# Staging the last weight matrix of a fused attention and gated-MLP kernel in three buffers instead of one

## The chip, the cores and the metric

The kernel runs on one core of one Trainium2 chip. The metric is the device time in microseconds (us) of that core. TensorE is called PE in the profile, VectorE DVE, ScalarE ACT, GpSimd POOL and SyncE SP; PEld is TensorE's weight load.

## The reference

Causal attention over 8 batches and 8 heads (576 positions, head size 64), with a bias from the running sum of `max(s, 0)`, and behind it a gated MLP. With `x` the attention's output, 512 wide:

```python
h = np.maximum(x @ w_in, 0.0)              # 512 -> 1024
u, v = h[..., :512], h[..., 512:]
v_n = (v - mean(v)) / sqrt(var(v) + 1e-6)  # over the last axis
v_s = einsum('ts,bsd->btd', w_spatial, v_n) + b_spatial[None, :, None]
return (u * v_s) @ w_out                   # 512 -> 512
```

The weights `w_in` and `w_out` arrive as 64-bit floats. This document is about how `w_out` (512 x 512) gets into the form in which the last product reads it.

## The kernel before, in words

**The precision scheme.** A matrix product is made of three float16 products: each operand is held as a high part and a low part (the rest that the high part leaves, also float16), and high x high, high x low and low x high are summed in one PSUM bank. So `w_out` is held as `wo1` (high) and `wo2` (low), each four pieces of 128 rows.

**How a piece of w_out is made** (`load_wout`, lines 496 to 498). `fetch_w64` brings 128 x 512 64-bit numbers (512 KB) by a DMA that is issued from GpSimd's queue. `split_w64` (lines 469 to 478) then works on the two 32-bit halves: three integer operations on VectorE build a 32-bit float in a scratch tile `t`; ScalarE squares the upper word in place, so that a fourth VectorE operation can zero tiny numbers; `split_w` (lines 458 to 464) makes the high part on ScalarE. For the low part `split_w` has two ways, chosen by its last argument: with True, one VectorE operation multiplies and subtracts; with False, ScalarE scales the scratch in place and GpSimd subtracts. `load_wout` passes False.

**The tiles.** The 64-bit words of all four pieces are staged in the one tile `WST`, which before that serves a piece of `w_in` and, in `load_wtail`, a small bias row. The scratch `t` comes from `OB`, a ring of two tiles that is handed out in program order: the four pieces of `w_spatial` (`load_wsp`) use it just before the pieces of `w_out`, the output tiles of the MLP after them. `PH` is a ring of two tiles that hold softmax weights of the pairs of heads from number 8 on (in the profile they are called `pb`); before that nothing uses them here.

**What orders the work.** There is no loop order in the program: every operation is recorded with a priority, and a planner in the kernel file (`Recorder.forward`, line 199) plays the whole program through with estimated durations, on each engine always taking the ready operation with the lowest priority number. The result is a fixed order for each engine's queue, and on the chip each engine goes through its queue in that order and waits where something is not there yet. An operation that has nothing to wait for can be placed long before its number suggests, as soon as its engine has nothing lower to do. [...] The numbers: the attention scores of pair p (two heads) start at 2p - 1, its weighted sum at 2p + 2.7; the MLP of batch b is 29 units between 8b + 10.3 and 8b + 18.3; evacuations of the MLP come 3 earlier than their unit. `w_in` has 0.1 to 7.5, `w_spatial` 8.3 to 9.7, and the four pieces of `w_out` 10.6, 11.7, 12.8 and 13.9.

**The last product of a batch** (lines 863 to 883) has 8 units of 12 matmuls, for 128 output rows and half of the positions each. A unit takes the next of three PSUM banks `psM` in turn and is cut into two halves of 6 matmuls: the first half needs the pieces 0 and 1 of `w_out`, the second half the pieces 2 and 3. The same three banks, in the same turn, serve the other three products of the MLP, the transposes of softmax weights (`ident,p` in the profile) and the division by the softmax sums (`over`, `smx` and `rb` in the profile, pairs 0 to 7), without which the MLP of the next batch has no input.

Of the kernel before, what the change touches and what calls it, by code (L numbers as in the profile page):

```python
# [10 lines left out]
U32 = mybir.dt.uint32  # L11
# [288 lines left out]
def attn_gated_mlp(ctx, tc, qkT, v, s, w_in, w_spT, b_sp, w_out, outT):  # L300
    nc = tc.nc
    P = 128
# [7 lines left out]
    w_out = w_out.bitcast(U32)  # L310
    NF = FF // 2
# [18 lines left out]
    def tiles(n, shape, dt, name):  # L330
        return [cp.tile(shape, dt, name=f"{name}{i}") for i in range(n)]
# [19 lines left out]
    WST = tiles(1, [P, 2 * NF], U32, "wst")[0]  # L351
# [3 lines left out]
    PH = Ring(tiles(2, [P, 2 * 1280], F16, "pb"))  # L355
# [11 lines left out]
    wo1, wo2 = (cp.tile([P, FC, DM], F16, name=n) for n in ("wo1", "wo2"))  # L367
# [90 lines left out]
    def split_w(dst1, dst2, raw, sc, dve):  # L458
        A.activation(dst1, raw, AF.Copy, bias=0.0, scale=sc)
        if dve:  # L460
            V.scalar_tensor_tensor(out=dst2, in0=raw, scalar=sc, in1=dst1, op0=ALU.mult, op1=ALU.subtract)
            return
        A.activation(raw, raw, AF.Copy, bias=0.0, scale=sc)
        G.tensor_tensor(out=dst2, in0=raw, in1=dst1, op=ALU.subtract)

    def fetch_w64(src, st):
        G.dma_start(out=st, in_=src)

    def split_w64(dst1, dst2, st, t, dve):
        st = st.rearrange("p (f two) -> p f two", two=2)  # L470
        lo, hi = st[:, :, 0], st[:, :, 1]
        V.tensor_scalar(t, hi, 0x07FFFFFF, 3, op0=ALU.bitwise_and, op1=ALU.logical_shift_left)
        V.scalar_tensor_tensor(out=t, in0=hi, scalar=0xC0000000, in1=t, op0=ALU.bitwise_and, op1=ALU.bitwise_or)
        V.scalar_tensor_tensor(out=t, in0=lo, scalar=29, in1=t, op0=ALU.logical_shift_right, op1=ALU.bitwise_or)
        sq, tf = hi.bitcast(F32), t.bitcast(F32)
        A.activation(sq, sq, AF.Square, bias=0.0, scale=1.0)
        V.scalar_tensor_tensor(out=tf, in0=sq, scalar=2.0 ** -30, in1=tf, op0=ALU.is_ge, op1=ALU.mult)
        split_w(dst1, dst2, tf, SW, dve)
# [9 lines left out]
    def wt():  # L488
        return OB.next()[:, 0:NF].bitcast(U32)

    def load_win(hf, c):
        t = HV.next().bitcast(U32) if hf else wt()
        split_w64(win1[:, c, hf * NF:(hf + 1) * NF], win2[:, c, hf * NF:(hf + 1) * NF], STG[hf, c], t,
                  c < (2 if hf else 1))

    def load_wout(c):
        fetch_w64(w_out[c * P:c * P + P], WST)
        split_w64(wo1[:, c], wo2[:, c], WST, wt(), False)

    def load_wsp(c):  # L500
        st = OB.next()
# [388 lines left out]
    def at(pos, d, fn, *args):  # L890
        plan.append((pos, len(plan), d, fn, args))
# [42 lines left out]
    for c in range(KC):  # L934
        at(0.1 + 0.5 * c if c < 2 else 1.5 + 0.1 * c, 0, fetch_win, 1, c)
        at(2.1 + 0.5 * c if c < 3 else 4.05, 0, fetch_win, 0, c)
        at(2 + 1.0 * c, 0, load_win, 1, c)
        at(6 + 0.5 * c, 0, load_win, 0, c)
        at(8.5 + 0.4 * c, 0, load_wsp, c)
        at(10.6 + 1.1 * c, 0, load_wout, c)  # L940
    at(8.3, 0, load_wtail)
    for p in range(NP):
        units([2 * p + k / 3 for k in range(6)], ATT, s_pass, p)
# [46 lines left out]
```

## Time and profile before

| | |
|---|---|
| median of 3 runs | 661.55 us (661.17 to 663.3) |
| profiled execution | 661.49 us |
| its span in the trace | 659.8 us |
| PE busy | 620.2 us, 94% |
| DVE busy | 527.2 us, 80% |
| ACT busy | 505.9 us, 77% |
| POOL busy | 214.3 us, 32% |
| DMA, mean rate | 161 GB/s |

The profiled execution spends 1.69 us outside its span. The profile cuts the span into 40 slices of 16.5 us and gives the busy tenths of each engine and the clock that TensorE was granted. The kernel records all its operations through one helper, so nearly every row carries the line number 279: rows are told apart by the names of their tiles (`psM<-g,wo` is a matmul of the last product; `wst`, `ob`, `wo` belong to the making of `w_out`). An entry such as [1.68 <-ACT q] behind a row is the time that the engine sat idle before it, and what released it.

### The profile page before, as it was taken

To read this page: it belongs to the slowest core of one execution; us is meant where nothing else is said; L and a number is where in the kernel's file an instruction comes from. 1 tells how busy PE (TensorE), PEld (TensorE's weight loads), DVE (VectorE), ACT (ScalarE), POOL (GpSimd) and SP (SyncE) were. 2 spreads that over 40 slices of the span, in tenths; PEclk is the share of its full clock that TensorE was granted. 3 is DMA by queue.
4 is the path that set the end of the run, shared out by engine and by line. 5 is a ranking of instruction groups with operands and counts; after the bars stand their busy time and mean duration, and the time that the engine had idled before them with its cause. 6 is when DMAs were issued, how large, how long until landed. Compare 5 with 4: busy or idle time off the path is not lost.

```text
span 659.8 us, 15930 instructions
## 1 busy us (share of the span) xinstructions
PE 620.2 (94%) x5785; PEld 426.7 (65%) x5785; DVE 527.2 (80%) x1527; ACT 505.9 (77%) x1336; POOL 214.3 (32%) x326
## 2 busy tenths in 40 slices
PE   6983779999689999999999999999999999999997
PEld 3542455777456776677757775677667775777675
DVE  8788787868867898999889988999899988880440
ACT  3895987988866889798879888788889897862422
POOL 9746545542332413432243323323243112000200
PEclk9995999999799999999999999999999999999999
DMA  8854355342992899898998999998999895762001
GB/s 222 266 180 125 111 144 151 104 122 87 197 240 57 198 193 243 176 176 183 241 208 180 197 210 206 180 197 186 238 174 204 160 209 92 107 116 74 12 2 72
DMA packets 185574, 106.20 MB, mean 161 GB/s; under 512 B 162025, under 2 KB 165271, under 8 KB 185497
## 3 DMA queue, kind: packets, MB, share of 16 engines
q1 hardware_dynamic: 176201, 70.14, 53.4%
q0 software_dynamic: 9296, 35.07, 18.4%
q8 instruction: 45, 0.74, 0.5%
q14 instruction: 32, 0.26, 0.1%
HBM read 37.48 MB, written 9.66 MB: 71 GB/s over the span
## 4 chain that ended last, share of the span: by engine, by line
PE 82%; ACT 7%; DVE 5%; DMA 2%; issue 2%; POOL 2%; SPq 0%; ACTq 0%; DVEq 0%; POOLq 0%
PE psM L279 60%; PE psS L279 12%; PE psV L279 8%; ACT p L279 2%; PE psT L279 2%; DVE psS L279 1%; DMA raw<-in_qkT_dram 1%; ACT pT L279 1%; DMA st<-st 1%; POOL QB L279 1%; DVE hv L279 1%; ACT q L279 1%; ACT KA L279 1%; DVE g L279 1%; DVE mx L279 1%
## 5 line engine op out<-in xcount | busy, mean ns | idle before, releaser
L279 DVE CUSTOM_DVE_ANT_0 psS<-psS,mb 128x128 f32<-128x128 f32 (+1 forms) x320 | 155.2, 497 | 29.3 <-PE psS L279 24.7
L279 ACT ACTIVATE p<-psS,mx 128x128 f32<-128x128 f32 (+3 forms) x256 | 134.4, 530 | 42.1 <-DVE mx L279 38.8
L279 POOL TENSOR_TENSOR QB<-raw,KA 128x288 f16<-128x288 f32 x116 | 89.8, 797 | 142.1 <-ACT KA L279 141.4
L279 DVE SCALAR_TENSOR_TENSOR pb<-p,sm,pb 128x384 f16<-128x384 f32 x192 | 103.5, 572 | 6.9 <-ACT pb L279 6.2
L279 PE MATMUL psM<-ws,vn 128*128 128x288 f16 x768 | 106.0, 286 | 0.0
L279 PE MATMUL psM<-g,wo 128*128 128x288 f16 x768 | 103.3, 289 | 0.5 <-POOL wo L279 0.5
L279 PE MATMUL psM<-xt,win 128*128 128x288 f16 x768 | 101.4, 286 | 0.1
L279 PE MATMUL psM<-win,xt 128*128 128x512 f16 (+1 forms) x576 | 100.7, 344 | 0.0
L279 ACT ACTIVATE pb<-p,sm 128x384 f16<-128x384 f32 x192 | 96.2, 560 | 1.0 <-ACT p L279 0.5
L279 PEld LDWEIGHTS <-wo 128*128 128x128 f16 x768 | 74.9, 99 | 26.2 <-issue 2.8
L279 PEld LDWEIGHTS <-win 128*128 128x128 f16 x768 | 73.9, 98 | 23.4 <-issue 2.1
L279 PE MATMUL psS<-KA,QA 128*128 128x128 f16 (+1 forms) x348 | 80.4, 306 | 9.0 <-ACT p L279 5.4
L279 PEld LDWEIGHTS <-vn 128*128 128x128 f16 x768 | 74.0, 98 | 22.7 <-issue 1.6
L279 PE MATMUL psS<-KB,QB 128*128 128x128 f16 (+1 forms) x348 | 87.2, 300 | 0.0
L279 PEld LDWEIGHTS <-xt 128*128 128x128 f16 (+1 forms) x576 | 46.4, 102 | 45.5 <-issue 4.2
L279 PE MATMUL psV<-pT,vv 128*64 128x384 f16 (+5 forms) x880 | 64.5, 298 | 5.6 <-DVE hv L279 5.6
L279 POOL TENSOR_SCALAR rs<-mv 128x1 f32<-128x1 f32 x40 | 12.7, 318 | 146.4 <-DVE mv L279 145.5
L279 PEld LDWEIGHTS <-vv 128*64 128x64 f16 x1440 | 45.5, 111 | 13.8 <-issue 6.1
L279 ACT ACTIVATION_READ_ACCUMULATOR p<-psS,mx 128x1 f32 x256 | 52.3, 204 | 0.0
L279 ACT CAST g<-g 128x288 f16<-128x288 f32 x64 | 27.5, 431 | 27.6 <-DVE g L279 27.4
L279 DVE DVE_READ_ACCUMULATOR2_ANT mx<- 128x1 f32 x320 | 44.8, 140 | 0.0
L279 PEld LDWEIGHTS <-QA 128*128 128x128 f16 x348 | 28.9, 101 | 21.5 <-issue 14.3
(124 smaller groups left out, 951.6 us busy)
## 6 DMA issues: line engine op xcount, KB each, us to landing
raw<-in_qkT_dram POOLq DMA_DIRECT2D x29, 576.0 KB, 5.3
out_dram<-ob SPq DMA_DIRECT2D x32, 288.0 KB
vraw<-in_v_dram POOLq DMA_DIRECT2D x12, 512.0 KB, 5.7
QA<-KA SPq DMA_DIRECT2D x29, 144.0 KB
KB<-KA SPq DMA_DIRECT2D x29, 144.0 KB
KB<-QB SPq DMA_DIRECT2D x29, 144.0 KB
QB<-KA SPq DMA_DIRECT2D x29, 144.0 KB
vv<-in_v_dram POOLq DMA_DIRECT2D x4, 512.0 KB, 7.5
```

The costliest lines, as they stand in the source:

```text
L279: getattr(eng, method)(*args, **kw)
```

## The change

It moves the transfers of `w_out` into a function of their own, gives the four pieces three staging buffers (pieces 0 and 3 the first tile of `PH`, piece 1 the second, piece 2 `WST`), gives the transfers the numbers 10, 10.3, 10.6 and 10.9 and the conversions 10.5, 11.2, 11.9 and 12.6, and makes all four low parts on VectorE.

```diff
+    def stage_out(c):
+        return WST if c == 2 else PH.tiles[c % 3].bitcast(U32)[:, 0:2 * NF]
+
+    def fetch_wout(c):
+        fetch_w64(w_out[c * P:c * P + P], stage_out(c))
+
     def load_wout(c):
-        fetch_w64(w_out[c * P:c * P + P], WST)
-        split_w64(wo1[:, c], wo2[:, c], WST, wt(), False)
+        split_w64(wo1[:, c], wo2[:, c], stage_out(c), wt(), True)
...
-        at(10.6 + 1.1 * c, 0, load_wout, c)
+        at(10 + 0.3 * c, 0, fetch_wout, c)
+        at(10.5 + 0.7 * c, 0, load_wout, c)
```

## The prediction

> **What bounds the kernel now.** I read the page's strip first. Each digit is 16.5 us; the eleventh and twelfth slices (165 to 198 us) are the last with a PE below 9 before the end, and the eleventh has a lowered clock.
>
> ```profile
> PE   6983779999689999999999999999999999999997
> ...
> PEclk9995999999799999999999999999999999999999
> ```
>
> Then the windows: busy us (and instructions) of PE, PEld, DVE, ACT and POOL, the granted clock, the DMA share and GB/s.
>
> ```profile
> 98.00:159.00 61.00, 60.69 (x494) 42.94 (x493) 47.81 (x136) 49.77 (x131) 27.61 (x42) 1.00 0.45 126
> 159.00:186.00 27.00, 20.05 (x158) 12.67 (x155) 22.63 (x69) 23.57 (x60) 10.92 (x14) 0.87 0.78 165
> 186.20:655.70 469.50, 469.39 (x4619) 328.70 (x4618) 376.73 (x1110) 359.30 (x944) 114.61 (x185) 1.00 0.78 162
> ```
>
> PE is full from 98 to 159 and has 0.11 us of idle time in the 469.5 us from 186.2 to the end. So what is saved before 186 moves the end one for one, unless a new idle time opens behind it. Between lie 27 us with 6.95 us idle. The timeline of PE there:
>
> ```profile
> 159.09 2.37 PE L279 MATMUL psM<-g,wo 128*128 128x288 f16 x18
> ...
> 167.30 0.38 PE L279 MATMUL psS<-KA,QA 128*128 128x512 f16 x1 [1.68 <-ACT q L279]
> ...
> 171.23 0.26 PE L279 MATMUL psS<-KA,QA 128*128 128x128 f16 x1 [2.88 <-ACT p L279]
> ...
> 174.80 5.71 PE L279 MATMUL psM<-g,wo 128*128 128x288 f16 x37 [0.51 <-POOL wo L279]
> ...
> 185.64 0.38 PE L279 MATMUL psS<-KA,QA 128*128 128x512 f16 x1 [1.80 <-ACT q L279]
> ...
> 186.16 1.50 PE L279 MATMUL psM<-win,xt 128*64 128x256 f16 x24
> ```
>
> The 18 matmuls at 159.09 are three first halves of units (3 x 6); they leave all three psM banks half summed. The waits that follow name attention (ACT q, ACT p), but that is only what came next in PE's queue. What is missing is the rest of the last product, as the windows of tile psM alone show:
>
> ```profile
> 161.50:172.80 11.30, 0.00 (x0) 0.00 (x0) 0.00 (x0) 0.00 (x0) 0.88 0.62 140
> ```
>
> For 11.3 us no instruction touches those banks. The piece that they wait for is seen on POOL:
>
> ```profile
> 104.32 0.60 POOL L279 DMA_DIRECT2D wst<-in_w_out_dram  x1
> ...
> 127.27 0.61 POOL L279 DMA_DIRECT2D wst<-in_w_out_dram  x1
> ...
> 129.96 1.15 POOL L279 TENSOR_TENSOR wo<-ob,wo 128x512 f16<-128x512 f32 x1 [0.44 <-ACT ob L279]
> ...
> 141.98 0.53 POOL L279 DMA_DIRECT2D wst<-in_w_out_dram  x1 [6.40 <-DVE ob L279]
> ...
> 155.98 0.53 POOL L279 DMA_DIRECT2D wst<-in_w_out_dram  x1 [6.58 <-DVE ob L279]
> 157.54 1.16 POOL L279 TENSOR_TENSOR wo<-ob,wo 128x512 f16<-128x512 f32 x1 [1.04 <-ACT ob L279]
> ...
> 173.11 1.63 POOL L279 TENSOR_TENSOR wo<-ob,wo 128x512 f16<-128x512 f32 x1 [4.28 <-ACT ob L279]
> ```
>
> One staging tile makes a relay: each transfer waits for the conversion before it, and the fourth low part ends at 174.74. The chain of waits runs through it and straight on into PE:
>
> ```profile
> 173.11 1.64 POOL wo L279
> ...
> 174.80 7.62 PE psM L279 x53
> ```
>
> The lowered clock sits behind the same gap:
>
> ```profile
> 168.00:171.00 3.00, 0.35 (x2) 0.16 (x2) 3.00 (x8) 3.00 (x9) 0.57 (x1) 0.84 0.92 160
> 171.00:174.00 3.00, 2.77 (x11) 1.34 (x10) 3.00 (x8) 2.16 (x7) 0.89 (x1) 0.50 0.88 270
> 174.00:177.00 3.00, 2.49 (x12) 1.43 (x11) 2.67 (x11) 2.73 (x9) 2.02 (x3) 0.52 1.16 207
> ```
>
> PE worked 2.77 us at 0.50 and 2.49 us at 0.52; at full clock that is 2.77 x 0.50 + 2.49 x 0.48 = 2.6 us less.
>
> **The change, part by part.**
>
> *Transfers 0 and 1* go to tiles that nothing has used, so they wait for nothing, and the planner will put them at POOL's first moment without a lower number. All transfers of w_in go before them; I place them behind the last of these:
>
> ```profile
> 27.84 0.53 POOL L279 DMA_DIRECT2D u<-in_w_in_dram  x1
> 40.26 1.87 POOL L279 TENSOR_TENSOR QB<-raw,KA 128x288 f16<-128x288 f32 x2 [11.90 <-ACT KA L279]
> ```
>
> ```profile
> 30.00:34.00 4.00, 3.44 (x19) 2.08 (x20) 3.35 (x15) 3.75 (x13) 0.00 (x0) 1.00 1.03 341
> 34.00:42.00 8.00, 6.80 (x38) 3.83 (x37) 6.83 (x26) 7.96 (x24) 1.74 (x2) 1.00 0.36 131
> ```
>
> Two issues of 0.6 us lie in 11.9 us of idle POOL, and 1.05 MB at the 341 GB/s seen there is 3.1 us, against (1 - 0.36) x 8 = 5.1 us of free DMA time from 34 to 42. Cost: nothing. If that cover is gone they stand in front of a later load of raw, with up to 2 x (0.6 + 3.9) = 9.0 us (3.9 is the median landing in the rows of tile wst below). On POOL they are moved past some forty-five instructions; on SP's queue nothing moves. *Transfer 2* needs only WST, as the first transfer does today. *Transfer 3* waits for piece 0's conversion; behind it in POOL's queue stand low parts of keys and queries (QB), now as before behind two such waits (6.40 + 6.58 us); one goes.
>
> *Conversions.* Their start is then set by the scratch ring, whose tiles come free with the third and fourth piece of w_spatial:
>
> ```profile
> 117.13 0.75 DVE L279 SCALAR_TENSOR_TENSOR ws<-ob,ws 128x576 f16<-128x576 f32 x1
> 117.91 0.43 DVE L279 TENSOR_SCALAR ob<-wst 128x512 uint32<-128x512 uint32 x1
> ...
> 120.19 0.75 DVE L279 SCALAR_TENSOR_TENSOR ws<-ob,ws 128x576 f16<-128x576 f32 x1
> ...
> 125.67 1.06 DVE L279 SCALAR_TENSOR_TENSOR ob<-wst,ob 128x512 f32<-128x512 f32 x1 [0.78 <-ACT wst L279]
> ...
> 151.40 0.42 DVE L279 TENSOR_SCALAR ob<-wst 128x512 uint32<-128x512 uint32 x1
> ```
>
> Piece 0 cannot start earlier than today's 117.91; its low part ends today at 129.96 + 1.15 = 131.1, 13.2 us later. Piece 1 can start at 120.9. Transfer 3 goes out when piece 0's fourth VectorE step is done, 125.67 + 1.06, near 127. Today the third transfer's issue at 141.98 and the start of its conversion at 151.40 are 9.4 us apart, the first's (104.32 to 117.91) 13.6; a conversion takes 7.3 (151.40 to 157.54 + 1.16) to 13.2. So the last piece is ready between 127 + 9.4 + 7.3 = 144 and 127 + 13.6 + 13.2 = 154, against 159.1 when PE asks first. Both ends are in time.
>
> *The low parts.* Prices, from the groups by form and from tile wst between 100 and 180 us (minimum, median, maximum ns):
>
> ```profile
> L279 POOL TENSOR_TENSOR wo<-ob,wo 128x512 f16<-128x512 f32 x4 | 5.1, 1276 | 7.5 <-ACT ob L279 7.5
> ...
> L279 ACT ACTIVATE ob<-ob 128x512 f32<-128x512 f32 x7 | 4.4, 630 | 0.1
> ...
> L279 DVE SCALAR_TENSOR_TENSOR win<-ob,win 128x512 f16<-128x512 f32 x1 | 0.7, 693 | 0.7 <-ACT win L279 0.7
> ```
>
> ```profile
> L279 DVE SCALAR_TENSOR_TENSOR ob<-wst,ob x12: 672/689/1477, 121.5 to 170.9; 128x512 uint32<-128x512 uint32 x8, 128x512 f32<-128x512 f32 x4
> ...
> DMA to landing us min/median/max: 3.8/3.9/4.2
> ```
>
> POOL loses 5.1 us, ACT 4 x 0.63 = 2.5; DVE gains 4 x 0.69 = 2.8 (the same form), at most 4 x 1.48 = 5.9. None of it is on PE's path while PE is full, and DVE has 61 - 47.81 = 13.2 us free from 98 to 159. If that room is gone, attention falls behind (third rival).
>
> [...]
>
> *What PE gains.* With w_out there, 78 of the 96 matmuls (some 10 us at 18 in 2.37) fill the two gaps, 1.68 + 2.88, and the wait for wo, 0.51, goes; without a long gap the clock stays up, 2.6. The wait of 1.80 at 185.64 is attention's own pace, and I count 0 of it (bounds 0 and 1.80). Sum: 1.68 + 2.88 + 0.51 + 2.6 = 7.7 us. Behind it PE needs the next MLP 7.7 us earlier, at 178.5. Its inputs hang on psM banks (division for pair 7), which come free earlier too:
>
> ```profile
> 164.33 0.75 PE L279 MATMUL psT<-pTt,vv 128*64 128x64 f32 x20
> ...
> 180.35 0.60 PE L279 MATMUL psM<-ident,smx 128*128 128x128 f32 x4
> ```
>
> The sums over values of pair 7 end at 165.08, and from the division's transposes at 180.35 to 186.16 today's path took 5.8, so 170.9 is possible: 7.6 us of slack.
>
> Against the profiled execution (661.49 us, span and 1.69 around it): 661.49 - 7.7 = 653.8; the median of the runs is 0.06 higher, so 653.9.
>
> **The rivals.**
>
> *Only part of the gain.* DVE and ACT were full from 168 to 171 (3.00 of 3.00 us each), so attention may be what holds PE in any order. Then the gain is what the fourth conversion stops taking from DVE: 0.43 + 3 x 0.69 = 2.5 us: 659.0. Against it: behind 186 DVE is busy 376.73 of 469.50 us, which lets it catch up, and PE has other work.
>
> *No change.* The last piece still comes late because the planner, which orders by estimates, puts the conversion behind attention; or the two early transfers lie in front of a load at 40 to 60 us, where PE is short of work, and eat the gain (653.9 + 9.0 = 662.9 at the most). 661.5 to 662.9.
>
> *Slower: VectorE is crowded between 118 and 159.* Three conversions stand there now, 3 x (0.43 + 3 x 0.69) = 7.5 us; then four with low parts, 4 x (0.43 + 4 x 0.69) = 12.8, and if every one of the longer steps is stretched to the slowest (16 x 1.48 + 4 x 0.43) 25.4. That is 5 to 18 us more in 13.2 us of room. The slack of 7.6 absorbs it; beyond that the next MLP starts late and PE stands idle, with a lowered clock again. At 17.9: 10.3 idle and 2.6 of clock give 653.9 + 12.9 = 666.8. It decides from 7.6 + 7.7 - 2.6 = 12.7 us of lateness. Against it: most steps in that row are near 689 ns.
>
> **How the numbers follow.** The forecast 0.62 (own range 651 to 657: the 1.80, and small new waits), part of the gain 0.14, no change 0.11, slower 0.13. Everything above 661.55 x 0.003 = 2.0 us can be told from no change. Faster is the first two, 0.76; same 0.11; slower 0.13. The range takes in the part gain and the lower end of no change: 650.5 to 662, with 0.05 left out below and 0.14 above.
>
> **What would show it.** Right: the four transfers of w_out on POOL with two near 28 us and none waiting 6 us for DVE ob; the last write to wo before 159; psM matmuls of g,wo without the 11.3 us pause; clock 1.00 from 160 to 190; PE's next MLP (win,xt) near 178; DVE busy about 2.8 us more. Wrong: a last wo after 159, a new gap on PE before or after that stage, or a start-up (40 to 64 us) that is longer than now.

## The result, and the profile after

| | before | after |
|---|---|---|
| median | 661.28 us (660.52 to 663.31, 14 executions) | 671.55 us (660.95 to 676.73, 14 executions) |
| ratio after / before | | 1.0054 (95% interval 1.0035 to 1.0073) |
| profiled execution | 661.49 us, span 659.8 | 663.51 us, span 661.4 |

The change makes the kernel slower, by 0.54% or 3.6 us in the ratio and by 10.3 us in the medians, where 653.9 us was forecast. Executions that lie more than 1.5% above the fastest of their kernel, eight of these 14, are left out of the ratios here and below, while medians are over all of them, which is why the two can differ. The profiled execution is 2.0 us longer than that of before, so the trace shows about half of the ratio's loss and a fifth of the medians'.

The strip of the page after, each digit 16.5 us: the dent in the eleventh and twelfth slices is gone, the one in the fourth is deeper (0 instead of 3), and the seventeenth (264 to 280 us) has a new, shallow one.

```profile
PE   7980779999999999899999999999999999999997
...
PEclk8995999999999999999999999999999999999999
```

The windows after (columns as in the prediction):

```profile
48.00:72.00 24.00, 6.90 (x54) 4.00 (x53) 14.87 (x21) 11.06 (x20) 14.39 (x19) 0.64 0.50 138
...
98.00:159.00 61.00, 60.43 (x514) 41.42 (x513) 51.94 (x145) 49.69 (x132) 27.29 (x38) 1.00 0.38 109
159.00:186.00 27.00, 26.68 (x246) 19.69 (x245) 21.88 (x66) 23.84 (x65) 8.99 (x11) 1.00 0.65 147
186.20:657.20 471.00, 466.70 (x4578) 325.51 (x4576) 377.39 (x1119) 358.35 (x948) 112.30 (x186) 1.00 0.79 164
```

and of the kernel before the one window that the prediction did not show:

```profile
48.00:72.00 24.00, 10.75 (x80) 6.31 (x79) 20.90 (x42) 14.81 (x36) 13.11 (x15) 0.72 0.44 127
```

From 159 to 186 PE is busy 26.68 of 27 us at full clock (before 20.05 at 0.87): the gain that was forecast there has come, and the wait of 1.80 us that the sum counted as nothing is gone too. It is given back twice. Between 48 and 72 PE does 6.90 us of work instead of 10.75, at a lower clock (from 48 to 98 it does 25.74 instead of 31.03). And behind 186, where PE had 0.11 us of idle time, it now has 471.00 - 466.70 = 4.30.

The start-up on PE, first the kernel before, then after (the view after ends inside its second row, so that row counts 16 of 20 matmuls):

```profile
53.99 1.12 PE L279 MATMUL psM<-ident,smx 128*128 128x128 f32 x4 [4.46 <-POOL smx L279]
60.71 4.11 PE L279 MATMUL psV<-pT,vv 128*64 128x384 f32 x20 [5.60 <-DVE hv L279]
```

```profile
55.63 1.12 PE L279 MATMUL psM<-ident,smx 128*128 128x128 f32 x4 [6.81 <-POOL smx L279]
66.64 3.53 PE L279 MATMUL psV<-pT,vv 128*64 128x384 f32 x16 [9.89 <-DVE hv L279]
```

The transposes for a division (`ident,smx`) come 1.6 us later, the next sums over values 5.9 us later. Between the two stands ScalarE's copy `rb`. The kernel before has it at 58.76; after, ScalarE's queue has conversions of `w_in` in front of it, which wait themselves:

```profile
58.76 0.59 ACT L279 COPY rb<-psM 128x512 f32<-128x512 f32 x1
```

```profile
61.30 0.63 ACT L279 ACTIVATE win<-ob 128x512 f16<-128x512 f32 x1 [4.32 <-DVE ob L279]
61.97 0.63 ACT L279 ACTIVATE ob<-ob 128x512 f32<-128x512 f32 x1
62.50 0.64 ACT L279 ACTIVATE u<-u 128x512 f32<-128x512 f32 x1
63.89 0.63 ACT L279 ACTIVATE win<-ob 128x512 f16<-128x512 f32 x1 [0.76 <-DVE ob L279]
...
65.21 0.58 ACT L279 COPY rb<-psM 128x512 f32<-128x512 f32 x1
```

What the first of them waits for stands in VectorE's queue behind a step that took 3.84 us, where the same operation took 0.68 at 50.49. It ends just after the four subtractions that GpSimd ran beside it (58.88 and 58.33):

```profile
55.04 3.84 DVE L279 SCALAR_TENSOR_TENSOR ob<-u,ob 128x512 uint32<-128x512 uint32 x1
```

```profile
55.55 2.78 POOL L279 TENSOR_TENSOR QB<-raw,KA 128x288 f16<-128x288 f32 x4
```

The kernel before has such a long step there too (2.89 us at 53.40), so this alone does not make the difference; e16 tests what stands ahead of `rb`.

`w_out` itself is where the prediction wanted it: two transfers early, no wait between them, the last low part done at 149.1 us, 10 us before PE used to ask.

```profile
42.17 1.09 POOL L279 DMA_DIRECT2D pb<-in_w_out_dram  x2
...
110.81 0.60 POOL L279 DMA_DIRECT2D wst<-in_w_out_dram  x1
123.89 0.59 POOL L279 DMA_DIRECT2D pb<-in_w_out_dram  x1
```

```profile
148.40 0.68 DVE L279 SCALAR_TENSOR_TENSOR wo<-ob,wo 128x512 f16<-128x512 f32 x1
```

The largest new wait behind 186, on PE, VectorE and SyncE's queue after the change:

```profile
275.35 1.63 PE L279 MATMUL psM<-xt,win 128*128 128x288 f16 x12 [2.13 <-ACT hv L279]
```

```profile
259.48 5.95 SPq L279 DMA_TRANSPOSE pT<-pb  x1
265.88 1.10 SPq L279 DMA_DIRECT2D st<-st  x2
```

```profile
271.68 0.21 DVE L279 BATCH_NORM_AGGREGATE mv<-st 128x2 f32<-128x12 f32 x1 [2.21 <-DMA st<-st]
```

PE waits for ScalarE, which waits for VectorE's statistics of the normalization, and these wait for two small copies `st<-st`, which stood in SyncE's queue behind a transpose of 5.95 us. In the kernel before the copies stand ahead of that transpose:

```profile
259.97 1.22 SPq L279 DMA_DIRECT2D st<-st  x2
262.07 4.41 SPq L279 DMA_TRANSPOSE pT<-pb  x1
...
268.25 0.20 DVE L279 BATCH_NORM_AGGREGATE mv<-st 128x2 f32<-128x12 f32 x1
```

The changed order issues the copies 3.6 us before VectorE is free for what needs them (265.88, and 271.68 - 2.21); in the order before it was 8.3 us (259.97 to 268.25), and nothing waited. The length of the transpose ahead of them does not decide it: in the profile of e14 (below), whose order is the same at this place, the transpose took 5.38 us, the copies were issued at 265.01, and VectorE went on at 269.68 without a wait; in e8 it took 5.36 and VectorE waited 2.56. What differs is how soon the copies land: VectorE went on 5.8 us after their issue in the changed kernel (271.68 - 265.88), 6.8 us in e8 (272.52 - 265.74), and in e14 they took 4.7 us at most (269.68 - 265.01). Why it differs no run here shows.

None of these operations belongs to `w_out`. They moved because the planner, given other numbers, buffers and engines for the operations of `w_out`, wrote a new order for all engines.

### The profile page after: what moved, and what is told of

It reads as the page before. It is cut to its first block, busy times and chain, and to the rows that moved or that the text cites. A ratio compares the mean times of both kernels' runs of the same rounds, so it can differ in the third digit from the quotient of the medians.

```text
span 661.4 us, 15922 instructions
## 1 busy us (share of the span) xinstructions
PE 620.1 (94%) x5785; PEld 426.9 (65%) x5785; DVE 524.8 (79%) x1531; ACT 501.8 (76%) x1332; POOL 208.4 (32%) x322
## 5 line engine op out<-in xcount | busy, mean ns | idle before, releaser
L279 DVE SCALAR_TENSOR_TENSOR pb<-p,sm,pb 128x384 f16<-128x384 f32 x192 | 101.5, 563 | 6.8 <-ACT pb L279 6.2
```

The source lines that it names most:

```text
L279: getattr(eng, method)(*args, **kw)
```

## The experiments

The first four undo or do one part each and let the planner order the work anew. They rest on the theory that the forecast gain is there and a longer start-up eats it; the rivals are that new waits come up behind 186, and that VectorE's low parts cost time. From e5 on, with two exceptions (e7, e8), the order is held fixed and one thing is changed in it by hand. Each kernel ran beside the kernel before on the same chip.

**e1: the first transfers may not come early.** A dependence that only the planner sees puts transfers 0 and 1 behind the last small transfer of the bias row, next to transfer 2 (105 us in its trace).

```diff
@@ load_wtail
             Y.dma_start(out=wx2[TAIL + i:TAIL + i + 1], in_=bp[:, i])
+        gate.append(R.ops[-1])
@@ fetch_wout
         fetch_w64(w_out[c * P:c * P + P], stage_out(c))
+        R.ops[-1].preds[gate[0]] = True
```

> The changed kernel, with one line more for the planner: the transfers of pieces 0 and 1 may be placed only after load_wtail, as the transfer into WST is. Staging in three buffers, numbers and low parts on VectorE stay. Theory A (the two transfers at 42 us make the start-up longer, by the planner's order or by their traffic): the sums over values of pair 1 start near 60.7 us as in the kernel before (66.6 in the changed one), PE stays full from 159 to 186, and the time is 652 to 655 us. Theory B (the start-up is longer for another reason, or small waits behind 186 cost the gain in any case): 658 us or more.

Measured: median 662.14 us (656.54 to 671.31), ratio 1.0006 (0.998 to 1.0031). The start-up's waits are those of the kernel before (values of pair 1 at 60.80, wait 5.61), and PE is busy 30.68 of 31 us from 159 to 190. By the ratios e1 is 0.48% faster than the changed kernel (1.0006 against 1.0054), some 3 us, and still the forecast gain does not come out: the time is on theory B's side.

**e2: the planner doesn't count the early transfers.** They stay on POOL near 42 us with all their bytes.

```diff
         fetch_w64(w_out[c * P:c * P + P], stage_out(c))
+        if c < 2:
+            R.ops[-1].dma = R.ops[-1].occ = 0.0
```

> The changed kernel, in which the planner counts nothing for the two early transfers (neither their issue nor their bytes); on the chip they run at the same place in POOL's queue, at 42 us, with all their bytes. Theory A1 (it is the planner's order: its model of the transfer queue holds POOL back and so puts conversions of w_in ahead of the division's rb on ScalarE): the start-up is as before, sums over values of pair 1 near 60.7 to 61.5 us, time 652 to 656. Theory A2 (it is the traffic of 1 MB at 42 to 50 us on the chip): the sums start at 65 us or later, time 660 to 664 or more.

Measured: 666.07 us (656.38 to 668.79), ratio 0.9992 (0.9966 to 1.0018). The start-up's waits are again those of the kernel before, with both transfers in place:

```profile
55.01 1.12 PE L279 MATMUL psM<-ident,smx 128*128 128x128 f32 x4 [4.46 <-POOL smx L279]
61.72 4.47 PE L279 MATMUL psV<-pT,vv 128*64 128x384 f32 x20 [5.60 <-DVE hv L279]
```

The longer start-up is thus not the traffic; it is the order that the planner writes when it counts the traffic. The time that theory A1 forecast with it (652 to 656) did not come: behind 186 this order has a wait of its own, of 2.91 us, with a clock of 0.57 behind it (last section).

**e3 and e4: the engine of the low parts, planned anew.** e3 is the changed kernel with `split_w64(..., False)`, e4 the kernel before with `True`.

> The changed kernel with the low parts of w_out made on ScalarE and GpSimd as before (last argument False). Theory A (start-up order or traffic decides): start-up as in the changed kernel, sums of pair 1 near 66.6 us, time within 3 us of the changed kernel's. [...]

> The kernel before with the low parts of w_out on VectorE alone; one staging buffer and the old numbers. Theory A: the relay stays, each conversion is shorter by ScalarE's scaling (0.63) and by 1.28 - 0.69 us, so the last low part ends 1 to 2 us earlier and the time is 659 to 661.5 us. Theory C (VectorE crowded): 662 to 665 us.

Measured: e3 671.85 us (663.9 to 676.56, 4 executions), start-up as in the changed kernel, so the low parts alone don't undo the loss; e4 665.89 us (664.61 to 667.2), ratio 1.0068 (1.0054 to 1.0082), pause from 161 to 173 still there. e4 lies outside both ranges of its expectation, nearer to theory C's: one flag costs the kernel before 4.4 us. Whether that is VectorE's time or again the order, e4 can't tell. That is why the order is held from here on.

**e5: the order of the kernel before, only memory and transfers changed.** The planner plans with the one tile `WST`; what is issued uses three buffers, with transfers 1 and 2 right behind transfer 0 and transfer 3 right behind the conversion of piece 0.

```diff
+    def stage_out(c):
+        return PH.tiles[c - 1].bitcast(U32)[:, 0:2 * NF] if c in (1, 2) else WST
...
+    def earlier(order):
+        for c in range(1, 4):
+            order.remove(pieces[c][0])
+        k = order.index(pieces[0][0]) + 1
+        order[k:k] = [pieces[1][0], pieces[2][0]]
+        k = max(order.index(o) for o in pieces[0]) + 1
+        order[k:k] = [pieces[3][0]]
+        return order
```

> The kernel before with its own order of work on every engine, written out as the planner made it for one staging tile; only the memory changes: piece 0 of w_out is staged in WST, pieces 1 and 2 in the two pb buffers, piece 3 in WST again, and on POOL's queue the transfers of pieces 1 and 2 stand right behind that of piece 0 (104.3 us), that of piece 3 right behind the last conversion of piece 0. Low parts stay on POOL. Theory L (the late piece was worth what the prediction said, and what the changed kernel loses comes from the planner's new order): 652.5 to 655.5 us, no wait of several us between 161 and 173, granted clock 1.00 from 159 to 190, less than 1 us of idle PE after 186, spread of a few us as before. Theory C (the pause from 161 to 173 let attention's preparation run ahead, and without it PE meets waits of the same total later): 657 to 662 us, with 3 us or more of idle PE after 186, behind ACT or DVE, and a spread of 6 us or more.

Measured: 661.11 us (660.6 to 663.77), ratio 1.0003 (0.999 to 1.0016). Nothing. GpSimd, PE and VectorE in e5:

```profile
105.69 1.05 POOL L279 DMA_DIRECT2D pb<-in_w_out_dram  x2
...
131.54 0.57 POOL L279 DMA_DIRECT2D wst<-in_w_out_dram  x1
```

```profile
167.77 0.38 PE L279 MATMUL psS<-KA,QA 128*128 128x512 f16 x1 [1.68 <-ACT q L279]
...
171.69 0.27 PE L279 MATMUL psS<-KA,QA 128*128 128x128 f16 x1 [2.88 <-ACT p L279]
```

```profile
167.09 0.75 DVE L279 TENSOR_SCALAR ob<-wst 128x512 uint32<-128x512 uint32 x1
```

The fourth transfer is issued 24 us earlier than in the kernel before, and its conversion still starts at 167.09 (before: 166.6), because in VectorE's queue it stands behind attention's work of that moment. PE's two waits have the same length to the hundredth, 1.68 and 2.88. The late transfer, on which the prediction rests, held up nothing that was not held up by the order already. Theory L's time fails. The time lies in theory C's range, but its signs are missing: there is no new wait behind 186 (PE is busy 109.98 of 110 us from 190 to 300), and the spread is 3 us. The pause has simply stayed.

**e6: the same order, low parts on VectorE in the places where GpSimd had them.**

```diff
+        cp.calls, lo.calls = [], x.ops[0].calls
...
+        for p in pieces:
+            p[-1].eng = "vector"
```

> The kernel of e5 with the four low parts of w_out on VectorE, each in the place of the order where it stood on POOL, without ScalarE's copy ahead of it; everything else in the same order. Theory L (order alone matters): within 1 us of e5 (652 to 656). Theory D (e4's 4.4 us are VectorE's extra time, four times 0.7 us, in front of attention's evacuations): 3 to 5 us above e5, with longer idle times of PE behind DVE between 120 and 190 us.

Measured: 662.45 us (661.54 to 664.77), ratio 1.0014 (1.0002 to 1.0026), 1.3 us above e5 in the median, between the two theories and nearer to L. So in a fixed order the low parts on VectorE cost about a microsecond at most (the intervals of e5 and e6 overlap), and most of e4's 4.4 us was order.

**e7: e1 with the low parts on GpSimd, planned anew.** Its order is, of those planned with three buffers, the one nearest to the kernel before; e4's, with one buffer, is nearer still.

> The kernel of e1 (the planner must place the first transfers behind the bias's last transfer) with the low parts left on POOL: of the planned kernels the one whose order is nearest to the kernel before. Theory L: start-up as before (values of pair 1 wait 5.6 us), no pause from 161 to 173, and 653 to 659 us depending on what the new order does after 186. Theory C: 657 to 664 with new waits on ACT and DVE after 186. If the low parts on VectorE were what cost e1 its gain: 652 to 656.

Measured: 656.37 us (654.53 to 661.72), ratio 0.9936 (0.9917 to 0.9954): faster than both kernels. PE is busy 30.68 of 31 us from 159 to 190, and behind 186 only two waits are over 0.3 us (0.32 and 0.69), so theory L's side.

**e8: the changed kernel again, for a second profile.**

> The changed kernel once more, for a second profile of it. Theory L and C both: 661 to 677 us. If an execution above 668 is caught, the extra time against the profile at 663.51 lies (theory P, the planner's long start-up) ahead of 98 us as lower clock and idle PE, or (theory C) after 186 as waits on ACT and DVE of 0.5 to 3 us.

Measured: 666.86 us, so no execution above 668 was caught. Its start-up is nearly that of the first profile (PE's two waits 6.27 and 10.48 us instead of 6.81 and 9.89, values of pair 1 at 66.58 instead of 66.64); it differs by one more wait behind a DMA. ScalarE and PE:

```profile
401.15 0.71 ACT L279 ACTIVATE ob<-psM 128x288 f32<-128x288 f32 x2 [2.24 <-DMA out_dram<-ob]
```

```profile
401.91 0.81 PE L279 MATMUL psM<-win,xt 128*128 128x512 f16 x3 [2.11 <-ACT ob L279]
```

**e9 to e11: the last piece's conversion moved up by hand.** e9 is e5 with the conversion of piece 3 right behind that of piece 2 in the queues of VectorE, ScalarE and GpSimd; e10 is the same move in the kernel before with its one staging tile; in e11 it stands behind piece 1. PE's queue is untouched in all three.

```diff
...
+        last, k = pieces[3], 0
+        for o in last[1:]:
+            order.remove(o)
+        k = order.index(pieces[2][-1]) + 1
+        for o in last[1:]:
+            k = max([k] + [order.index(x) + 1 for x in o.preds if x in order])
+            order[k:k] = [o]
+            k += 1
...
```

> The kernel of e5 (own order of the kernel before, three staging buffers, early transfers, low parts on POOL) with one thing moved: the conversion of the last piece of w_out (four steps on VectorE, three on ScalarE, one on GpSimd) stands in the queues right behind that of the piece before it, where the trace of e5 has about 156 to 161 us, instead of behind the maxima and exponentials of the next pair (167 to 174 us). Theory Q (the place in the in-order queues, not the transfer, held the last piece back): the pause of PE from 165 to 174 goes, last write to wo near 161, clock 1.00 from 160 to 190, and 653 to 657 us. Theory C (attention holds PE in any order there): the waits on ACT q and ACT p stay in sum at 4 us or more, or come back later; 659 to 662 us.

> The kernel before, with its one staging tile and its own order, and only that same move of the last piece's conversion in the queues of VectorE, ScalarE and GpSimd. The transfer of the last piece still waits for the conversion of piece 2 and lands near 160 us. Theory Q with the transfer next in line: VectorE, ScalarE stand still behind the transfer for a few us, last write to wo near 165 to 168, and 656 to 661 us. If the transfer is of no matter: as e9. Theory C: 660 to 663 us.

> As e9, but the last piece's conversion stands right behind that of piece 1 (about 143 to 148 us in the trace of e5). Theory Q: 653 to 657 us, within 1.5 us of e9, since both are ready when PE asks or nearly so. Theory C: 659 to 662 us.

Measured: e9 666.15 us (ratio 1.0068, 1.0051 to 1.0086), e10 666.85 (1.0086, 1.007 to 1.0101), e11 665.93 (1.0066, 1.0049 to 1.0083). All are slower by 5 to 6 us in the medians, above the ranges of both theories. So theory Q falls, and theory C is right that attention holds PE there, though not in its time. PE in e9:

```profile
164.66 3.46 PE L279 MATMUL psM<-g,wo 128*128 128x288 f16 x18 [3.46 <-ACT rbt L279]
...
173.78 0.38 PE L279 MATMUL psS<-KA,QA 128*128 128x512 f16 x1 [0.96 <-ACT q L279]
...
177.15 0.27 PE L279 MATMUL psS<-KA,QA 128*128 128x128 f16 x1 [2.33 <-ACT p L279]
...
178.81 7.28 PE L279 MATMUL psM<-g,wo 128*128 128x288 f16 x42
```

All of `w_out` is there by 165.4 (the last low part on GpSimd starts at 164.2), and yet the matmuls that could fill the gaps at 173 and 177 run at 178.81: in PE's queue they stand behind the scores, and PE does not pass them. What the move did was to put three ScalarE steps in front of copies (`rbt`) for which PE waits 3.46 us (5.25 in e10; in e11 PE waits 3.39 us at 152 for a copy `pT`). The pause was not a missing piece; it was written into PE's own queue. The gain came only in runs with another order of that queue (e7, e12, e13).

**e12: the order of e7, with the low parts on VectorE in place.** It has the change's buffers and engines, late transfers, and e7's order.

```diff
...
+    def low_parts_on_vector(order):
+        for op in lows:
+            op.eng = "vector"
+        return order
...
```

> The kernel of e7 (656.37 us) in its own order, with the four low parts of w_out on VectorE, each in the place where it stood on GpSimd, and without ScalarE's copies. e1, which differs from it in the planner's order alone, took 662.14. Theory L (what e1 lost against e7 is the planner's other order): 656 to 658.5 us. Theory D (VectorE's four steps cost it by themselves): 660 to 663 us.

Measured: 655.4 us (654.55 to 657.42), ratio 0.9913 (0.9898 to 0.9928), the lowest median of all. PE in e12:

```profile
160.79 1.63 PE L279 MATMUL psM<-g,wo 128*128 128x288 f16 x12
...
162.69 3.10 PE L279 MATMUL psM<-g,wo 128*128 128x288 f16 x24
...
178.68 2.46 PE L279 MATMUL psM<-win,xt 128*128 128x512 f16 x27
```

Here the units of the last product stand between the scores, and the next MLP (`win,xt`) starts at 178.68. e1 has the same instructions in the order that the planner writes when it knows of VectorE's low parts: 662.14 us, ratio 1.0006. The difference to 0.9913, 0.93% or 6 us, is order.

**e13 and e14: the early transfers, in two fixed orders.** e13 is e12 with transfers 0 and 1 moved up on GpSimd's queue to where the change has them: it issues every instruction of the changed kernel. e14 is the changed kernel's order with the same two moved down to transfer 2; its lines:

```diff
...
+        for op in fetches[:2]:
+            order.remove(op)
+        k = order.index(fetches[2])
+        order[k:k] = fetches[:2]
...
```

> The kernel of e12 (655.4 us) in its own order, with only transfers 0 and 1 of w_out moved up on GpSimd's queue to where the changed kernel has them, behind the low parts of keys at 40.3 us and ahead of the load of values at 42.1. It then issues the changed kernel's instructions, all of them, into the same buffers and with the same early transfers; only the order on the engines is another. Theory O (order alone): 655 to 658 us, start-up as in e12. Theory T (the two early transfers delay a load that the start-up waits for): 658 to 664 us, with the values of pair 1 starting later than 60.7.

> The changed kernel in its own order, with only transfers 0 and 1 moved down on GpSimd's queue, directly ahead of transfer 2 (about 111 us). Theory O: 667 to 674 us as the changed kernel, values of pair 1 still start at 66 to 67 us. Theory T: 660 to 666 us, and they start at 61 to 63.

Measured: e13 656.43 us (655.61 to 658.58), ratio 0.9924 (0.9904 to 0.9943); e14 669.63 (661.52 to 735.2), ratio 1.0036 (1.0014 to 1.0057). PE in e13, where both transfers are issued from 42.07 on:

```profile
61.54 4.42 PE L279 MATMUL psV<-pT,vv 128*64 128x384 f32 x20 [5.61 <-DVE hv L279]
```

The values of pair 1 start 0.8 us later than in e12 (60.71), with the same wait, 5.61, and the intervals of the two ratios overlap. In e14 they start at 66.68 although the transfers are gone from there, and its ratio overlaps with the changed kernel's. So the transfers cost 0.8 us at that place and nothing that the times can tell; theory O holds. e13 and e14 issue the same instructions and ran on one chip, 656.43 against 669.63 us. The same instructions in two orders, e13 and the changed kernel, are 1.3% apart by the ratios (0.9924 and 1.0054, 8.6 us) and 15.1 us in the medians.

**e15: the changed kernel's order, low parts back on GpSimd in place.** Where the low part stood on VectorE, ScalarE's copy and GpSimd's subtraction are issued.

> The changed kernel in its own order, with the four low parts on GpSimd and ScalarE's copy ahead of them, each in the place where they stood on VectorE. Theory O: 667 to 674 us. If the low parts on VectorE cost the changed kernel something by themselves: 660 to 667 us.

Measured: 672.09 us (666.25 to 676.69), ratio 1.0117 (1.0068 to 1.0165): no gain from GpSimd, as theory O has it. Its profile caught a long execution (674.75 us). SyncE's queue, ScalarE, VectorE and PE:

```profile
373.35 8.35 SPq L279 DMA_TRANSPOSE pT<-pb  x1
...
384.36 9.68 SPq L279 DMA_TRANSPOSE pT<-pb  x1
```

```profile
390.05 1.23 ACT L279 ACTIVATE pb<-p,sm 128x384 f16<-128x384 f32 x2 [3.70 <-DMA pT<-pb]
```

```profile
275.02 0.21 DVE L279 BATCH_NORM_AGGREGATE mv<-st 128x2 f32<-128x12 f32 x1 [3.27 <-DMA st<-st]
```

```profile
278.69 1.63 PE L279 MATMUL psM<-xt,win 128*128 128x288 f16 x12 [3.19 <-ACT hv L279]
...
394.07 0.64 PE L279 MATMUL psS<-KA,QA 128*64 128x512 f16 x2 [2.95 <-ACT p L279]
```

The wait at 275 in the first profile of the change is here 3.19 us instead of 2.13. Another of 2.95 us begins with ScalarE, which waits 3.70 us until a transpose has read the tile that it writes next. There are two such tiles in turn, and at 390.05 the transpose of 9.68 us was still in SyncE's queue (384.36 to 394.04), so the one that ScalarE waited for is the one before it, which had stood there for 8.35 us from 373.35. So the same order takes more or less time with how late its DMAs are done: it has places where one on SyncE's queue has no room left.

**e16: the changed kernel's order, the division of pair 1 moved up.** `rb` stands ahead of three of ScalarE's conversion steps, VectorE's product behind it ahead of one.

> The changed kernel in its own order, with the division of pair 1 moved up: ScalarE's copy of the sums ahead of three conversion steps of w_in (62.5 to 65.2 us in the trace) and VectorE's product ahead of one. Theory O with this as its first term: values of pair 1 start 2 to 3 us earlier (63.5 to 64.7 instead of 66.6), a half-clock window less in some executions, and the median 2 to 5 us lower, 666 to 670 us. If the start-up is not what sets the time: 671 to 672 us.

Measured: 665.65 us (659.4 to 673.79), ratio 1.003 (1.0004 to 1.0057).

```profile
64.10 4.54 PE L279 MATMUL psV<-pT,vv 128*64 128x384 f32 x20 [7.90 <-DVE hv L279]
```

The values of pair 1 start 2.5 us earlier (64.10 instead of 66.64), as theory O had it, so the copy's place is one cause of the longer start-up. What that is worth at the end is not settled: the median is 5.9 us below the changed kernel's, the ratio 0.24% (1.6 us), with overlapping intervals.

## Why the prediction was wrong, step by step

**What bounds the kernel now: the window was right, the cause wrong.** PE's loss did lie between 159 and 186. The step "What is missing is the rest of the last product", and the relay of transfers behind it, failed. The prediction itself says that the waits "name attention (ACT q, ACT p), but that is only what came next in PE's queue". That was the cause: PE did not pass what came next in its queue (in e9 matmuls whose piece was there at 165.4 ran at 178.81). e5 takes the relay away, e9 and e11 the late conversion too, and the waits on attention stay. Where the relay may matter is in the plan: the order made with it has the 78 matmuls behind the scores, the orders made with three buffers have them between (e12). No run that was planned anew changes the buffers without the numbers, so which of the two moved them is not shown.

**The sum of 7.7 us: nearly right, for an order that the change did not get.** In e12 and e13 the terms are there: no gap, full clock (1.00 from 159 to 175 in e12; in e13 12 matmuls of the last product take 1.63 us at 161.95 as at 177.40), in e12 the next MLP at 178.68 (forecast: near 178). That does not bear out the cause given for them, only the room on PE. They gain 661.07 - 655.4 = 5.7 and 661.56 - 656.43 = 5.1 us against the kernel before beside them. The 1.80 us that the sum left out went as well (in e12 PE is busy 26.75 of the 27 us from 159 to 186). Of what is missing to 7.7, 2.0 to 2.6 us, and of that 1.80, the trace of e12 shows waits of its own order, 0.43 us twice near 122, 0.32 at 140 and at 221, 0.67 and 0.87 near 345, together 3.0.

**Transfers 0 and 1: place wrong, price on the chip nearly right, consequence missed.** They went to 42.17, not 28, in front of loads of values. On the chip they cost 0.8 us at the values of pair 1 there (e13 against e12) and nothing that the times can tell, far from the 9.0 us "if that cover is gone". But the planner counts 512 KB each in its transfer queue, which it keeps at most 4 us ahead of the issuing engine (`link` in `Recorder.forward`), and what it re-ordered for that made the start-up 5.9 us longer at the values of pair 1 (e2, without the counting: 1.0). So "Cost: nothing" failed: PE has done 5.3 us less work by 98 us. The text named a longer start-up as a sign of being wrong; it was seen as a matter of traffic, not of order.

**Conversions: right.** The last piece was ready at 149.1, forecast 144 to 154, VectorE's steps `ob<-pb,ob` mostly at their short durations (median 685 ns, the longest 1339).

**Low parts on VectorE: right as a price, wrong as an edit.** In a fixed order they cost 1.3 us (e6 over e5) or gain 1.0 (e12 under e7), with overlapping intervals both times, and e15 is not faster than the change. After the change the four steps took 676 to 686 ns, 2.7 us in sum (forecast 2.8, at most 5.9). But changing the engine changes the plan: e1 against e12 is 6 us for that alone.

**"PE has 0.11 us of idle time in the 469.5 us from 186.2 to the end. So what is saved before 186 moves the end one for one, unless a new idle time opens behind it".** With "Cost: nothing" above, this is the step that carries the error in the sum. The 0.11 is a property of one order, not of the kernel. The new order has 4.30 us of idle time there in the profiled execution. Against the 6.63 us of idle time and 2.6 us of lowered clock that PE gained from 159 to 186 stand 5.3 us lost in the start-up and 4.2 us behind 186, which leaves nothing of the gain.

**The rivals.** "Only part of the gain" feared that attention holds PE in any order: it does in the order of the kernel before (e5, e9), and not in e12's. "No change" named the planner putting the conversion behind attention, which did not happen, and early transfers eating the gain, which happened in another way. "Slower" was VectorE crowded between 118 and 159: VectorE rose from 47.81 to 51.94 us of 61 there, and PE lost 0.26. The rival that was missing: any edit that the planner sees draws a new order for the whole program, and the order of the kernel before was a tight one.

**What stays open.** Why the times of the changed order lie 16 us apart (3 before): one thing that differs from profile to profile is shown, waits released by DMAs of SyncE's queue (near 275 us PE waits 2.13 us in the first profile, 2.48 in e8's, 3.19 in e15's and not at all in e14's), but no profile has an execution of the changed kernel above 666.86. e15's profile (674.75 us), in the same order but for the low parts, has 8.9 us of PE waits over 0.3 us behind 186, where the changed kernel's first has 3.7; what makes the DMAs late there is not known. Also open is which waits make the 6 us between e1 and e12; the profiled executions show 3.9 and 1.9 us of waits over 0.3 us behind 186.

## What to carry to other kernels

Where a planner writes a fixed order for each engine, an edit is two edits: the work itself and the new order of everything else. Hold the order (plan with the old dependences and costs, exchange only what is issued) to price the first, and look at several orders before the second is taken for a property of the change. Take a wait's releaser in an in-order queue at its word first: before you name something farther back as the cause, check that the engine's queue would let other work go ahead, because a piece that comes earlier is worth nothing to matmuls that stand behind the waiting one (in e9 it was there by 165.4, and they ran at 178.81).

## What the runs showed of the hardware

**The clock fell behind a wait of 2.91 us in e2, and not behind one of 3.19 in e15.** In e2 PE waited 2.91 us until 382.46, and its clock was 0.57 from 383 to 386 and 1.00 from 387 to 390:

```profile
379.00:382.40 3.40, 0.55 (x7) 0.23 (x6) 3.31 (x9) 2.96 (x11) 0.00 (x0) 1.00 1.24 175
383.00:386.00 3.00, 3.00 (x17) 1.82 (x16) 1.57 (x7) 2.57 (x9) 1.40 (x3) 0.57 0.98 173
387.00:390.00 3.00, 3.00 (x26) 2.25 (x23) 2.21 (x8) 2.23 (x7) 0.95 (x2) 1.00 1.24 212
```

The wait of 2.95 us in e15 was followed by 0.51 (394 to 400), that of 2.13 us at 275 in the changed kernel by 1.00 (276 to 280). The length of the wait alone does not decide it: behind the 3.19 us of e15 12 matmuls took 1.63 us, the same as behind the 2.13 us of the changed kernel; and both kernels have a wait of 1.55 us until 11.2 us, behind which the clock from 12 to 14 was 0.50 in the changed kernel and 1.00 in the one before. What else decides no run here shows.

**DMA transposes took from 2.9 to 9.7 us.** The same instruction stood in SyncE's queue for 2.9 us at the least and 9.68 at the most; the changed kernel, then e15 (minimum, median, maximum ns, first and last start):

```profile
L279 SPq DMA_TRANSPOSE pT<-pb x48: 2908/3468/5947, 169.4 to 590.9; - x48
```

```profile
L279 SPq DMA_TRANSPOSE pT<-pb x48: 2918/3422/9683, 171.7 to 601.9; - x48
```

The median hardly moves. Why single ones took so long no run here shows.
